# A gated-recurrence and feed-forward kernel on one core: the order of its first loads

## The chip, the cores and the metric

The kernel runs on one core of a Trainium2 chip. The time is device microseconds of that core, from one launch; the median of several runs is given. A core has TensorE for matrix products (its weight loads are counted apart), VectorE and ScalarE for elementwise work, GpSimd, and a sync engine that only issues transfers. ScalarE can issue transfers too, so there are two queues here: the sync queue and the ScalarE queue.

## The reference, cut to what matters

A recurrence with a complex gate for each step and feature, and then a feed-forward layer with a squared ReLU over its output:

```python
# q, k, v, a_re, a_im: (4, 8, 768, 48)    batch, heads, steps, features
mag = np.sqrt(a_re * a_re + a_im * a_im)
scale = np.minimum(mag, 0.999) / (mag + 1e-06)
a_re_n, a_im_n = (a_re * scale, a_im * scale)
for t in range(S):
    new_re = ar * S_re - ai * S_im          # ar, ai: the gates of step t
    new_im = ar * S_im + ai * S_re
    kv = np.einsum('bhd,bhe->bhde', k[:, :, t], v[:, :, t])
    S_re, S_im = (new_re + kv, new_im)
    y[:, :, t] = np.einsum('bhd,bhde->bhe', q[:, :, t], S_re)
...
x = np.ascontiguousarray(attn_out.transpose(0, 2, 1, 3)).reshape(B * S, H * D)   # 3072 x 384
h = np.maximum(x @ w_in, 0.0)               # w_in 384 x 2048
return (h * h @ w_out).astype(np.float32)   # w_out 2048 x 384
```

The weights arrive as 64-bit floats. The kernel gets them as pairs of 32-bit words and makes 32-bit floats of them itself.

## The kernel before, in words

**Tiling.** The steps are cut into 24 chunks of 128, and two chunks of different batches make a group, so there are 12 groups. Features lie on the partitions: the two heads of a pair take 48 partitions each (`rows`), and the 16 partitions left over in each half (`pads`, the gap rows) hold the fourth pair of heads, spread over three columns. So one tile `raw` of 128 partitions by 4 kinds (real gate, imaginary gate, query, key) by 768 holds all of a group. There is one `raw` for all groups: the next group's features can be loaded only when the present group's keys have been read out of it.

**Loads.** `load_parts` (L487) fills `raw`. For each chunk and each half it issues one large transfer into `rows` (L493) and then small ones into the gap rows (L498), one for each of the three columns. For the first group it is called twice, `l0.0` for the gates and `l0.1` for queries and keys, and with `l0.0` the second half goes out on the ScalarE queue (L490). Later groups are loaded whole, on the sync queue. `load_values` (L506) loads the values of a group, two transfers of 192 KB. `fetch` (L593) loads one of 16 blocks of weight words, six transfers for a block of the first weight matrix.

**Work of a group.** `make_operands` (L652) is a list of 22 steps, `o<group>.<step>`. Step 0 squares the gates on ScalarE (L683), and everything in the group follows from that: steps 1 and 2 turn the gates into another order, 4 and 5 take inverse roots, 8 to 11 make the limited gates (VectorE, L735), 6 turns the queries, 12 makes a negated copy on ScalarE (L743), 13 makes the running growth of the keys on VectorE, 14 turns the keys on ScalarE, 15 to 19 run products over blocks of steps on VectorE with some copies on ScalarE (18, the carries, L771), 20 makes the products for TensorE, and 21 copies gap rows to whole heads. `chunk` (L812) then is the recurrence of a chunk (`a` and `b`): scores (L841), keys turned (L848), scores masked by VectorE, sums of values (L867), the new state (L885). `F` and `H` are the first product of the feed-forward layer (L923) and its squared ReLU (L928, L929), `T`, `S`, `Z`, `R` the second (L939, L998), `s` stores.

**Weights.** `W` (`watch`, L580) squares a block of weight words on ScalarE to record its size (L582, L584); `D` (`weights`, L613) decodes it on VectorE in five passes (L569 to L576 and a sum). Three blocks of words can be held at once, so the fourth fetch waits for the first decode.

**The mask.** `turn_mask` (`M0`, L522) copies a triangular mask in another order on ScalarE, transposes it on TensorE and copies it back on ScalarE. Its reader is the masking of the first chunk's scores. Ahead of it on ScalarE stands a single small activation (L557), which brings the table of functions with it.

**Order.** The order on VectorE, TensorE, ScalarE and the sync queue is written out by hand: the string `FRONT` (L1031) names the steps from first to last, `follow` (L1125) carries them out, and each engine keeps that order among its own instructions. An engine whose next instruction waits does nothing behind it; that holds for transfers on a queue as well. GpSimd is not in the hand-written order. [...]

## Time and profile before

| | before |
|---|---|
| time, median of 3 runs | 719.07 us (718.33 to 721.44) |
| span of the profiled execution | 716.5 us |
| TensorE busy with products | 624.1 us (87%) |
| TensorE weight loads | 547.8 us (76%) |
| VectorE busy | 531.7 us (74%) |
| ScalarE busy | 368.6 us (51%) |
| data moved | 47.76 MB, 67 GB/s over the span |
| first squares on ScalarE begin | 18.47 us |
| first use of TensorE for a group | 57.84 us |

A share of the whole span is a mean over stages that have different limits, so the table alone does not say what one change is worth. A profile is read by stage: the slices show where an engine is full and where it is not, and within a stage the idle time before an instruction, with what ended it, shows what it waited for. Where times of a stage are given as three numbers in a row, such as 28.13 of 29.20, they are the busy time and the length of the stage.

### The profile page before, as it was taken

What the parts mean: (1) busy time and instruction counts of PE and PEld (TensorE: products, weight loads), DVE (VectorE), ACT (ScalarE), POOL (GpSimd) and SP (SyncE); (2) the same over time, 40 slices, a digit from 0 to 9 for tenths busy, and PEclk for the clock granted to TensorE, in tenths of its full rate; (3) what the DMA queues carried; (4) which work ended last, traced back from release to release, by engine and by line L of the source; (5) the groups of instructions that cost most, each with busy time, mean ns of one, the idle gap of its engine ahead of it and who ended that gap; (6) DMA issues with size and microseconds to landing.
All of it is one profiled execution on the core that took longest, in us unless ns stands there. A gap on an engine that the chain in (4) does not pass through costs nothing.

```text
span 716.5 us, 12546 instructions
## 1 busy us (share of the span) xinstructions
PE 624.1 (87%) x4955; PEld 547.8 (76%) x4955; DVE 531.7 (74%) x1045; ACT 368.6 (51%) x636; POOL 11.9 (2%) x36
## 2 busy tenths in 40 slices
PE   0005579899979999999999999999999999999995
PEld 0004468676558899998898998988988988989995
DVE  0599999999989697786975886886877868932120
ACT  1729378656536637628347367267276285240230
POOL 3000000000000000000000000000000000000000
PEclk9999789999999999999999999999999999999999
DMA  4596737375070152161331530720620610010101
GB/s 118 101 154 125 101 64 168 93 151 150 21 119 25 22 112 40 31 112 32 66 77 19 91 72 1 117 45 1 116 45 17 116 31 2 10 42 1 28 0 28
DMA packets 46277, 47.76 MB, mean 67 GB/s; under 512 B 6144, under 2 KB 41088, under 8 KB 46208
## 3 DMA queue, kind: packets, MB, share of 16 engines
q1 hardware_dynamic: 45696, 46.46, 33.6%
q8 instruction: 41, 0.67, 0.4%
q10 hardware_dynamic: 512, 0.39, 0.2%
q14 instruction: 28, 0.23, 0.1%
HBM read 36.18 MB, written 4.72 MB: 57 GB/s over the span
## 4 chain that ended last, share of the span: by engine, by line
PE 73%; DVE 13%; DMA 7%; SPq 3%; issue 1%; ACT 1%; ACTq 0%; DVEq 0%
PE h_ps L923 29%; PE o_ps L998 26%; PE a_ps L841 5%; PE o_ps L939 5%; DMA raw<-in_feat_dram 4%; PE y L867 2%; PE y L833 2%; DVE ab L478 2%; PE add L885 2%; PE tp L848 1%; DMA words<-in_moe_w_in_dram 1%; SPq L800 1%; DVE pr L478 1%; DVE w L478 1%; DVE qk L478 1%
## 5 line engine op out<-in xcount | busy, mean ns | idle before, releaser
L923 PE MATMUL h_ps<-x,w 128*128 128x256 f32 x1152 | 261.0, 384 | 8.8 <-DMA x<-x 8.0
L923 PEld LDWEIGHTS h_ps<-x,w 128*128 128x128 f32 x1152 | 219.1, 193 | 39.9 <-DMA x<-x 5.4
L998 PE MATMUL o_ps<-w,h 128*128 128x192 f32 x640 | 110.3, 328 | 0.0
L998 PEld LDWEIGHTS o_ps<-w,h 128*128 128x128 f32 x640 | 104.0, 190 | 2.2 <-issue 1.5
L928 ACT ACTIVATE h<-h_ps 128x512 f32<-128x512 f32 x96 | 57.6, 600 | 89.7 <-PE h_ps L923 86.2
L848 PE MATMUL tp<-ident,qk 128*128 128x128 f32 x120 | 22.2, 297 | 62.9 <-DVE qk L478 54.7
L848 PEld LDWEIGHTS tp<-ident,qk 128*128 128x128 f32 x120 | 14.7, 148 | 68.4 <-ACT size L584 55.0
L478 DVE TENSOR_TENSOR mix<-h 128x256 f32<-128x256 f32 x40 | 16.9, 422 | 62.7 <-ACT h L929 62.7
L929 ACT ACTIVATE h<-h 128x512 f32<-128x512 f32 x96 | 60.6, 631 | 3.0
L663 ACT ACTIVATE qk<-raw 128x768 f32<-128x768 f32 x24 | 36.8, 1534 | 36.0 <-DMA raw<-in_feat_dram 12.6
L998 PE MATMUL o_ps<-w_sum,mix 128*128 128x192 f32 x320 | 54.9, 329 | 0.0
L998 PEld LDWEIGHTS o_ps<-w_sum,mix 128*128 128x128 f32 x320 | 51.8, 190 | 1.4 <-issue 1.4
L478 DVE TENSOR_TENSOR pr<-ab 128x384 f32<-128x384 f32 x84 | 46.8, 557 | 2.3
L478 DVE TENSOR_TENSOR qk<-ab,qk 128x768 f32<-128x768 f32 x48 | 44.9, 956 | 0.8
L939 PE MATMUL o_ps<-w,h 128*128 128x384 f32 x128 | 42.3, 488 | 1.2 <-DVE w L478 0.6
L478 DVE TENSOR_TENSOR a<-a_ps,mask 128x512 f32<-128x512 f32 x48 | 30.9, 685 | 14.7 <-PE a_ps L841 14.7
L841 PE MATMUL a_ps<-qk 48*128 48x128 f32 x576 | 40.7, 291 | 0.0
L663 ACT ACTIVATE both<-z 128x768 f32<-128x768 f32 x24 | 37.1, 1563 | 5.7 <-DVE z L714 5.7
L841 PEld LDWEIGHTS a_ps<-qk 48*128 48x128 f32 x576 | 36.0, 197 | 4.4 <-issue 4.3
L663 ACT ACTIVATE ab<-raw 128x768 f32<-128x768 f32 x24 | 37.7, 1569 | 0.3 <-DVE qk L478 0.3
L939 PEld LDWEIGHTS o_ps<-w,h 128*128 128x128 f32 x128 | 24.2, 190 | 17.5 <-DVE w L478 1.3
L867 PE MATMUL y<-a,vt 128*64 128x128 f32 x384 | 29.0, 285 | 4.5 <-DVE a L478 4.3
(299 smaller groups left out, 817.4 us busy)
## 6 DMA issues: line engine op xcount, KB each, us to landing
raw<-in_feat_dram SPq DMA_DIRECT2D x44, 288.0 KB
words<-in_moe_w_out_dram SPq DMA_DIRECT2D x8, 768.0 KB
last<-qk SPq DMA_DIRECT2D x72, 64.5 KB
vt<-in_vtok_dram SPq DMA_DIRECT2D x24, 192.0 KB
out_dram<-o SPq DMA_DIRECT2D x24, 192.0 KB
raw<-in_feat_dram SPq DMA_DIRECT2D x132, 32.0 KB
words<-in_moe_w_in_dram SPq DMA_DIRECT2D x16, 192.0 KB
words<-in_moe_w_in_dram SPq DMA_DIRECT2D x32, 96.0 KB
```

What stands on the lines that cost most here:

```text
L478: nc.vector.tensor_tensor(out=out, in0=in0, in1=in1, op=op)
L663: nc.scalar.activation(out=out.rearrange("p c j n -> p c n j"), func=AF.Copy, in_=in_.rearrange("p c (n j) -> p c n j", j=L), **kwargs)
L833: nc.tensor.matmul(ys[p_ % 2][crossed(hh, p_), p_ // 2], lhsT=states[b][1 - c_seq % 2][rows(hh), c, p_], rhs=operand(c, p_, rows(hh)), sta ...
L841: nc.tensor.matmul(ps[hh][:, p_], lhsT=operand(2 + c, p_, rows(hh)), rhs=operand(c, p_, rows(hh)), start=(c == RE), stop=(c == IM))
L848: nc.tensor.transpose(tp[:, g], operands[gi][:, 2 + c, b, g, 0:C], ident)
L867: nc.tensor.matmul(tiles["y"][p_ % 2][crossed(hh, p_), p_ // 2], lhsT=v[:, at:at + ROWS], rhs=tiles["am"][hh][:, p_], start=(first and p_ ...
L885: nc.tensor.matmul(add[rr, c, p_], lhsT=kt[c][:, p_, rr], rhs=v[:, at:at + D], start=True, stop=True)
L923: nc.tensor.matmul(ps[:, j], lhsT=w1[:, g, (2 * f + j) * P:(2 * f + j + 1) * P], rhs=x_of[i][:, g], start=(g == 0), stop=(g == NG - 1))
L928: nc.scalar.activation(out=h, in_=h_ps[i, f], func=AF.Relu)
L929: nc.scalar.activation(out=h, in_=h, func=AF.Square)
L939: nc.tensor.matmul(o_of[i, b], lhsT=tokens_of(i, f, b)[:, j], rhs=w2[:, k], start=(k == 0), stop=(k == NFB - 1))
L998: nc.tensor.matmul(to, lhsT=x(k)[:, j], rhs=factor(z)[:, 2 * k + j], start=(z in (0, 1, 3) and k == j == 0), stop=(k == KH // 2 - 1 and j ...
```

## The change

The gates of the first group are to be first of all on both queues. For this the order string begins with `l0.0` in place of `M0`; the table's activation becomes `M0`, behind the transfers of `l0.0` on ScalarE, and the mask becomes `M1`, put behind the turned queries. The values of the first two groups, `v0` and `v1`, move behind the first fetch of weights. And the gap rows are loaded in as few transfers as the kinds and the columns allow: with two kinds asked for there are two transfers, one for each kind, in place of three, one for each column; with four kinds there are three as before. The rest of the order string is the same.

```diff
                     in_=feat[n, hh, :, parts, 0:NG].rearrange("d x g t -> d x (g t)"))
-                rest = feat[n, hh].rearrange("(r g) x p t -> g r x p t", g=NG)
-                for g in range(NG):
-                    queue.dma_start(out=raw[pads(hh), parts, b, g],
-                                   in_=rest[g, :, parts, NG])
+
+                gap = raw[pads(hh), parts, b]
+                rest = feat[n, hh].rearrange("(r g) x p t -> r x g p t", g=NG)[:, parts, :, NG]
+                for i in range(min(gap.shape[1:3])):
+                    at = (slice(None), i) if gap.shape[1] < NG else (slice(None), slice(None), i)
+                    queue.dma_start(out=gap[at], in_=rest[at])
...
-    def turn_mask():
+    def turn_mask(step):
+        if step == 0:
+
+            nc.scalar.activation(out=sums[:, 0:1], in_=tiny, func=AF.Abs_reciprocal_sqrt)
+            return
         nc.scalar.copy(out=mask.rearrange("p (j n) -> p n j", j=L),
                        in_=plain.rearrange("p (n j) -> p n j", j=L))
...
-    nc.scalar.activation(out=sums[:, 0:1], in_=tiny, func=AF.Abs_reciprocal_sqrt)
...
-        "M0 l0.0 v0 v1 l0.1 o0.0 o0.3 o0.1 o0.4 o0.5 o0.7 o0.2 f0 o0.8 o0.10 o0.9 o0.11 o0.6 W0 "
-        "f1 o0.13 o0.12 o0.15 o0.14 l1 o0.16 W1 o0.17 f2 D0 o0.18 o0.19 o1.6 o0.20 o1.0 f3 W2 "
-        "a0.1 o1.3 o1.1 o0.21 D1 o1.4 o1.5 o1.2 a0.2 o1.7 f4 a0.0 W3 D2 o1.8 o1.9 a0.3 a0.5 "
+        "l0.0 M0 l0.1 o0.0 o0.3 o0.1 o0.4 o0.5 o0.7 o0.2 f0 v0 v1 o0.8 o0.10 o0.9 o0.11 o0.6 M1 "
+        "W0 f1 o0.13 o0.12 o0.15 o0.14 l1 o0.16 W1 o0.17 f2 D0 o0.18 o0.19 o1.6 o0.20 o1.0 f3 "
+        "W2 a0.1 o1.3 o1.1 o0.21 D1 o1.4 o1.5 o1.2 a0.2 o1.7 f4 a0.0 W3 D2 o1.8 o1.9 a0.3 a0.5 "
...
-        "M": lambda _: turn_mask(),
+        "M": turn_mask,
```

## The prediction

> **What bounds the kernel now.** I read three views, in this order: the page's slices, to find where TensorE is not yet busy; the busy times by stage, to see which engine sets the pace of that stage; and the timeline of the start, to see what the pacing engine waits for.

> ```profile
> PE   0005579899979999999999999999999999999995
> DVE  0599999999989697786975886886877868932120
> DMA  4596737375070152161331530720620610010101
> ```

> Each digit is the busy share of one slice of 17.9 us. TensorE does nothing for three slices and is near full from the tenth on; VectorE is full from the third slice; in the first slice nearly nothing runs, and the DMA is busy less than half.

> The stages, in the columns PE, PEld, DVE, ACT, POOL, then granted clock, DMA share and GB/s:

> ```profile
> 0.00:18.40 18.40, 0.48 (x1) 0.18 (x1) 0.38 (x6) 2.15 (x4) 6.11 (x24) 1.00 0.42 116
> 18.40:28.60 10.20, 0.00 (x0) 0.00 (x0) 2.89 (x4) 9.54 (x10) 0.00 (x0) 1.00 0.81 160
> 28.60:57.80 29.20, 0.00 (x0) 0.00 (x0) 28.13 (x54) 12.83 (x23) 0.00 (x0) 1.00 0.71 114
> 57.80:91.20 33.40, 18.78 (x172) 15.35 (x172) 32.08 (x66) 20.77 (x40) 0.24 (x1) 0.86 0.68 113
> 240.00:716.50 476.50, 468.77 (x3834) 427.99 (x3830) 330.00 (x700) 230.62 (x403) 3.55 (x8) 1.00 0.25 47
> ```

> So there are four regimes, one after the other. To 18.4 us no engine works and data is awaited. From 18.4 to 28.6 ScalarE is busy 9.54 of 10.20 us. From 28.6 VectorE is, 28.13 of 29.20 and 32.08 of 33.40 us, and it stays so to about 154. From 240 on TensorE is, 468.77 of 476.50. A delay at the very start is handed through all of them. The timeline of the start (start, duration, engine, line, tiles; in brackets the idle time before it and its releaser; SPq and ACTq are transfers being issued):

> ```profile
> 0.81 0.39 SPq L493 DMA_DIRECT2D raw<-in_feat_dram  x1
> ...
> 3.16 0.37 ACT L527 COPY mask<-turned 128x128 f32<-128x128 f32 x1 [0.57 <-PE turned L526]
> ...
> 4.52 2.78 SPq L508 DMA_DIRECT2D vt<-in_vtok_dram  x4
> 5.39 0.39 ACTq L493 DMA_DIRECT2D raw<-in_feat_dram  x1
> ...
> 8.65 4.95 ACTq L498 DMA_DIRECT2D raw<-in_feat_dram  x3
> ...
> 13.64 0.44 ACTq L493 DMA_DIRECT2D raw<-in_feat_dram  x1
> 14.12 1.89 ACTq L498 DMA_DIRECT2D raw<-in_feat_dram  x3
> ...
> 18.47 1.48 ACT L683 ACTIVATE sq<-raw 128x1536 f32<-128x1536 f32 x1 [14.93 <-DMA raw<-in_feat_dram]
> ...
> 28.59 0.96 DVE L735 SCALAR_TENSOR_TENSOR both<-both 128x768 f32<-128x768 f32 x1 [3.60 <-ACT both L663]
> ...
> 29.66 0.88 ACT L582 ACTIVATE size<-words 128x768 bf16<-128x768 f32 x1
> ...
> 31.59 0.75 ACT L743 ACTIVATE ab<-ab 128x672 f32<-128x672 f32 x1
> ...
> 54.03 1.48 ACT L683 ACTIVATE sq<-raw 128x1536 f32<-128x1536 f32 x1 [2.75 <-DVE ab L478]
> ```

> The reader is to see that the first squares, at 18.47, waited 14.93 us for the gates (real and imaginary parts), and why these were late. The sync queue's half was issued from 0.81 on. The ScalarE queue's half was issued from 5.39 to 16.0, because that queue first had to finish the mask (3.53), and then found the value transfers and the queries and keys ahead of it. [...]

> [...] a gap transfer of 16 KB issued at 15.69 is what the squares at 18.47 wait for, 2.8 us for 16 KB. [...] the trace has the load at 1.28 us (0.81 to 2.09), and the activation follows at 2.10, [...] the trace shows a granted clock of 0.50 from 84 to 92 us, after TensorE had little to do.

> **The change, part by part.** *Order of the start.* The gates' 12 transfers (4 of 147 kB, 8 of 24.6 kB, 786 kB in all) are now first on both queues. By the issue pace of the sync queue (0.42 + 0.04 us each) four leave on each queue from 0.81 to 2.6; [...] In the view by single microseconds the DMA moved 23, 154, 80, 121 and 16 kB in the stretches from 1 to 6 us: 394 kB, which is the sync queue's half, 393 kB. So data starts about 1.9 us after the start. For the rate I take 180 GB/s (181, 183 and 176 GB/s at 8 to 11 us; about the same at 22 to 29): 786 kB take 4.4 us and end at 6.3. The tail to the landing is not shown for this order. It lies between nothing and the 2.4 us from the end of the last gap's issue (16.01) to the squares; I take 0.9, since the last gap transfers are issued some 1 us before the other data has passed. Squares at 7.2 us; 6.5 to 8.7 by the tail, 9.6 if the rate is only the 116 GB/s of the first stage (6.8 + 1.9 + 0.9). Gain 18.47 - 7.2 = 11.3 us.

> *Table load and first activation* now follow the six issues of the ScalarE queue. These end at about 5.0 [...], so the load ends at 6.3 and the activation at 6.5, under the last data's 7.2. Cost 0; at worst 0.5 if the sixth issue is late.

> *Fewer small transfers.* For the first group the gap rows take 2 instead of 3 transfers per half, chunk and pair of kinds: 8 fewer of 0.46 us on the queues and 8 fewer places. That is inside the 7.2 above for the gates; the queries' and keys' data ends at 1.9 + 1573 / 180 = 10.6, landed at about 12. They are wanted at 28.35 - 11.3 = 17.1: hidden. Later groups still use 3.

> *The mask* moves behind the queries and ahead of the first watch of weights. It costs 0.39 + 0.57 + 0.37 = 1.3 us on ScalarE (rows L523 and L527 with the wait for the transpose), and TensorE is idle then. Behind it on ScalarE stand the watch and the negated copy, which ran from 29.66 to 32.34; VectorE wants the negated copy only at 35.15. Slack 2.8, cost 1.3: hidden, 1.5 us left. The mask's own reader is at 68.46.

> *The values* go behind the first block of weights. Their first reader is the product at 69.20 (57.9 after the shift), and they land before 25. Hidden. Behind them on the sync queue stand the second block of weights and then the second group's features. Features, values and two blocks are 3.93 MB; at 180 GB/s from 1.9 us they end at 23.7, landed near 25. The second watch wants its block at 36.59 - 11.3 = 25.3, and what stands behind it on ScalarE (the carries) is wanted only at 45.35 - 11.3 = 34.0. The first block (1.9 + 2359 / 180 = 15.0, landed at 16 to 17) is wanted at 29.66 - 11.3 + 1.3 = 19.7.

> *The second group's features* wait for the keys' turned copy, which frees the tile: 36.81 before, 25.5 after. By then the earlier data is just done, where before the DMA stood idle from 30 to 36.8. If it is 2 us late, the slack of 2.75 us at 54.03 (its squares waited for VectorE, not for the features) takes it. From here on issue and work are tied to VectorE's own progress, so the whole schedule moves by 11.3. Sum: 719.07 - 11.3 + 0 = 707.8 us.

> **The rivals.** *Likeliest, full shift:* for it, ScalarE and VectorE are busy 94 to 96% from the squares on and TensorE's late stage is full, so nothing else binds. 707.8 us.
> *Part is eaten by the next data wait:* the first 30 us now need 3.93 MB without the pause that was there. If the squares start at 9.6 (116 GB/s), 8.9 us is gained; another 1 to 2 us could go to late blocks or late features beyond the 2.75 us of slack. 719.07 - 8.9 + 1.5 = 711.7 us. Against it: 160 GB/s were moved from 18.4 to 28.6.
> *Hidden anyway:* weights, not gates, pace the front, and VectorE meets them at the same time as before. 719 us. For it: DMA is at its limit around 38 to 56 us. Against it: up to 130 us one watch waited 0.4 us for weights, and their fetches are released by VectorE, so they move too.
> *Slower:* the second watch, behind the values, blocks ScalarE so long that the carries come late, or a half-clock stretch (the trace has 13.7 us of one, by the granted clocks from 80 to 96 us) falls elsewhere, over busy matmuls: up to 6.8 us. With the gain lost as well, 719 + 5 = 724 us. To undo the gain by the watch alone the second block would have to land near 43 us, 18 later than worked out.

> **How the numbers follow.** Full shift 0.70, part eaten 0.19, hidden 0.07, slower 0.04. The range has the full shift with its bounds (squares 6.5 to 8.7 and about 1.5 us of spread between runs, 718.33 to 721.44 before) and most of the part-eaten case: 705 to 712.5. Half a per cent is 3.6 us, so the first two cases are faster: 0.89; hidden gives the same, 0.07; slower 0.04.

> **What would show it.** Right: both queues' gate issues begin at 0.8; squares near 7; the gates' product on VectorE near 17.3; the first keys' transpose on TensorE near 46.5; the gap to the old trace stays at 11 us in the TensorE stage. Wrong: squares after 10; VectorE waits for the negated copy or for the second group's squares; a watch that holds ScalarE until the carries; a new half-clock stretch.

## The result, and the profile after

The changed kernel takes 712.27 us (median of 4 runs, 708.89 to 712.48) against 718.70 us (4 runs, 717.95 to 721.44): a ratio of 0.9893, 95% interval 0.9853 to 0.9932. Run again on a second chip it takes 707.77 us (6 runs, 707.17 to 711.85) against 719.94 us (27 runs), a ratio of 0.9833 [0.9805, 0.9861]. Both intervals lie clear of 1, so it is faster; but two medians of one program differ by 4.5 us. Most of what follows is about that: the early gain is the one that was worked out, within 0.6 us, and something later gives or takes 4 us.

Line numbers of the changed kernel are 3 to 4 higher than before from the gap rows' loads on (these are L501, were L498; the squares are L687, were L683), and the table's activation is L527, was L557. First the page's slices, one digit for each 17.8 us. PEclk, the granted TensorE clock in tenths, was not shown for before; its line there is `PEclk9999789999999999999999999999999999999999`.

```profile
PE   0025689999979999999999999999999999999995
...
DVE  1999989999798787996966886877868968932120
...
PEclk9999699999879999999999999999999999999998
DMA  5885582853351061341430620720611610010101
```

VectorE is full one slice earlier than before, and the DMA's second slice is an 8 where it was a 5. New is a dip of PEclk in slices 11 and 12, about 190 to 215 us, where before it is 9 throughout. The same four regimes, in the columns of the prediction (PE, PEld, DVE, ACT, POOL, clock, DMA share, GB/s):

```profile
0.00:7.00 7.00, 0.00 (x0) 0.00 (x0) 0.38 (x6) 1.49 (x2) 6.10 (x24) 1.00 0.48 125
7.00:18.00 11.00, 0.00 (x0) 0.00 (x0) 3.05 (x4) 9.69 (x10) 0.00 (x0) 1.00 0.59 132
18.00:47.00 29.00, 0.47 (x1) 0.18 (x1) 27.93 (x54) 13.54 (x25) 0.00 (x0) 1.00 0.92 164
229.00:711.00 482.00, 473.78 (x3909) 431.96 (x3907) 332.83 (x704) 235.29 (x411) 3.30 (x9) 0.99 0.25 47
```

The empty first regime has shrunk from 18.4 to some 7 us. The next two are as long and as full as they were: from the squares to the gates' product on VectorE it is 10.10 us, was 10.12 (the window of ScalarE, 9.69 of 11.00, begins 0.7 us before the squares), and VectorE is busy 27.93 of 29.00. The DMA share of the third went from 0.71 to 0.92, as the pause from 30 to 36.8 us (DMA share 0.00, the end of a wait of 10.2 us of the sync queue for ScalarE's turned keys) is gone. The timeline of the start of the changed kernel:

```profile
0.81 0.43 ACTq L493 DMA_DIRECT2D raw<-in_feat_dram  x1
...
4.17 1.21 ACTq L501 DMA_DIRECT2D raw<-in_feat_dram  x2
...
5.42 1.28 ACT L527 ACT_TABLE_LOAD   x1 [5.42 <-issue]
6.71 0.20 ACT L527 ACTIVATE sums<-tiny 128x1 f32<-128x1 f32 x1
7.72 1.48 ACT L687 ACTIVATE sq<-raw 128x1536 f32<-128x1536 f32 x1 [0.81 <-DMA raw<-in_feat_dram]
...
17.82 0.96 DVE L739 SCALAR_TENSOR_TENSOR both<-both 128x768 f32<-128x768 f32 x1 [3.59 <-ACT both L667]
...
22.07 0.75 ACT L747 ACTIVATE ab<-ab 128x672 f32<-128x672 f32 x1
...
29.19 0.90 ACT L586 ACTIVATE size<-words 128x768 bf16<-128x768 f32 x1 [3.17 <-DMA words<-in_moe_w_in_dram]
...
34.57 0.34 ACT L775 COPY carry<-ab 128x180 f32<-128x180 f32 x1 [3.34 <-DVE ab L478]
...
43.26 1.48 ACT L687 ACTIVATE sq<-raw 128x1536 f32<-128x1536 f32 x1 [1.60 <-DVE ab L478]
```

The squares begin at 7.72 instead of 18.47 us, 10.75 earlier, and the last data is the only thing they wait for, 0.81 us after the activation is done. The first turned keys on TensorE come at 47.10 instead of 57.87, 10.77 earlier. Their lines in the two timelines, before first, with the products that follow in the changed kernel:

```profile
57.87 0.87 PE L848 MATMUL tp<-ident,qk 128*128 128x128 f32 x3 [54.74 <-DVE qk L478]
...
47.10 0.87 PE L852 MATMUL tp<-ident,qk 128*128 128x128 f32 x3 [27.24 <-DVE qk L478]
47.90 2.93 PE L845 MATMUL a_ps<-qk 48*128 48x128 f32 x24
```

Followed product by product through both traces, TensorE is ahead of before by

```
at (us of before)   58 to 90       100     110    190    200    210    240 to the end
ahead by (us)       10.6 to 11.3   11.2    9.2    9.3    8.2    5.3    6.0
```

So the lead holds to 90 us, and then 1.5 us go near 105 and over 3 us near 205. In both places (95 and 196 us in the changed kernel) the granted clock falls to 0.50. One window of 3.41 us just ahead of the second place, and one within it, in the trace of the changed kernel:

```profile
186.14:189.55 3.41, 1.69 (x16) 0.90 (x18) 3.38 (x8) 1.23 (x4) 0.00 (x0) 1.00 0.36 91
...
192.97:196.38 3.41, 3.41 (x25) 2.52 (x25) 1.49 (x3) 0.65 (x2) 0.00 (x0) 0.50 1.02 177
```

TensorE has 1.69 us of work in the first (it waits for VectorE, 3.38 busy), and then runs at half clock while it has work all the time. The granted clock was 0.50 in these stretches (start and length in us, the one after the last product left out):

```
before                     81.9 (13.65)                215.1 (3.41)
changed                    70.1 (13.65)  94.0 (3.41)   189.6 (10.24)  210.0 (3.41)
changed, second profile    70.4 (13.65)  94.3 (3.41)   189.8 (6.83)   206.9 (6.83)
```

The stretch at 81.9 lies for the most part where TensorE has little to do (busy 4.65 of its first 10.24 us), and its counterpart in the changed kernel is at 70.1 (6.83 of 13.65). The others lie over busy products: TensorE is busy throughout those of the changed kernel, and 2.92 of 3.41 us in the one at 215.1 of before. The first products are slow in both kernels, too: the 24 products at 47.90 above take 2.93 us, as they do at 58.67 before, and the same kind of batch takes 1.61 us later (at 231.67, and before at 108.16). That they ran at half clock is an estimate, from such a batch that took 2.94 us at a granted 0.50 (further down): the profile has no record of the clock until 63.3 us (before: 75.1), so the 1.00 that it shows up to there is no measurement.

### The profile page after: what moved, and what is told of

It reads as the page before. It is cut to its first block, busy times and chain, and to the rows that moved or that the text cites. A ratio compares the mean times of both kernels' runs of the same rounds, so it can differ in the third digit from the quotient of the medians.

```text
span 710.7 us, 12538 instructions
## 1 busy us (share of the span) xinstructions
PE 629.6 (89%) x4955; PEld 551.7 (78%) x4955; DVE 531.9 (75%) x1045; ACT 368.6 (52%) x636; POOL 11.2 (2%) x36
## 4 chain that ended last, share of the span: by engine, by line
PE 77%; DVE 14%; DMA 4%; SPq 2%; issue 1%; ACT 0%; DVEq 0%; ACTq 0%
PE h_ps L927 31%; PE o_ps L1002 26%; PE a_ps L845 6%; PE o_ps L943 5%; PE y L871 3%; PE y L837 3%; DVE ab L478 3%; PE add L889 2%; PE tp L852 2%; DVE pr L478 2%; DVE decoded L575 1%; DVE decoded L580 1%; DVE qk L478 1%; DVE w L478 1%; DVE sq L753 1%
## 5 line engine op out<-in xcount | busy, mean ns | idle before, releaser
L932 ACT ACTIVATE h<-h_ps 128x512 f32<-128x512 f32 x96 | 57.6, 600 | 91.8 <-PE h_ps L927 88.8
L478 DVE TENSOR_TENSOR mix<-h 128x256 f32<-128x256 f32 x40 | 16.9, 422 | 62.5 <-ACT h L933 62.5
L667 ACT ACTIVATE qk<-raw 128x768 f32<-128x768 f32 x24 | 36.8, 1532 | 35.1 <-DMA raw<-in_feat_dram 14.4
L478 DVE TENSOR_TENSOR pr<-ab 128x384 f32<-128x384 f32 x84 | 46.7, 556 | 2.3
L478 DVE TENSOR_TENSOR qk<-ab,qk 128x768 f32<-128x768 f32 x48 | 44.9, 956 | 0.8
L478 DVE TENSOR_TENSOR a<-a_ps,mask 128x512 f32<-128x512 f32 x48 | 30.9, 685 | 17.8 <-PE a_ps L845 17.8
L845 PEld LDWEIGHTS a_ps<-qk 48*128 48x128 f32 x576 | 36.8, 200 | 4.6 <-issue 4.5
L943 PEld LDWEIGHTS o_ps<-w,h 128*128 128x128 f32 x128 | 24.1, 190 | 17.9 <-DVE w L478 1.5
```

Source lines behind the costliest of these rows:

```text
L478: nc.vector.tensor_tensor(out=out, in0=in0, in1=in1, op=op)
L667: nc.scalar.activation(out=out.rearrange("p c j n -> p c n j"), func=AF.Copy, in_=in_.rearrange("p c (n j) -> p c n j", j=L), **kwargs)
L845: nc.tensor.matmul(ps[hh][:, p_], lhsT=operand(2 + c, p_, rows(hh)), rhs=operand(c, p_, rows(hh)), start=(c == RE), stop=(c == IM))
L932: nc.scalar.activation(out=h, in_=h_ps[i, f], func=AF.Relu)
L943: nc.tensor.matmul(o_of[i, b], lhsT=tokens_of(i, f, b)[:, j], rhs=w2[:, k], start=(k == 0), stop=(k == NFB - 1))
```

## The experiments

Two questions: does the lead at 47 us come from the parts as worked out, and are the half-clock stretches what takes it back? The rivals for the loss: the changed loads themselves delay something later (a wait for data or for a buffer), or the runs simply scatter.

**The changed kernel again, on another chip.** No edit.

> The changed kernel itself, unedited, for the clock of each run. Half-clock theory (the gain at the start is 10.8 us, and TensorE at half clock around 95 and 190 us takes some 5 us back): runs differ, and the longer a run the lower its mean granted clock; 708 to 713 us, with each us of half clock in the late stretch costing about 0.4 us. Rival, data (late weights and the outputs' store take the gain back): all runs alike near 712 us, with no relation to the clock.

Measured: 707.77 us (711.28, 707.17, 707.21, 711.85, 707.61, 707.93). The six fall into two groups 4 us apart, and the granted clock recorded with each run goes with them: 0.983 to 0.986 for the four near 707.4, 0.975 and 0.972 for 711.28 and 711.85. The 27 runs of the kernel before beside them do the same:

```
                                clock 0.980 and over         below 0.980
kernel before, this chip        718.60 us (15 runs)          721.92 us (12 runs)
changed kernel, this chip       707.41 us (4 runs)           711.57 us (2 runs)
difference                      11.2                         10.35
kernel before, three chips      718.77 us (36 runs)          722.27 us (45 runs)
changed kernel, all ten runs    707.61 us (5 runs)           712.09 us (5 runs)
```

At like clock the change is worth 10.2 to 11.2 us. The first comparison had drawn three of four changed runs from the low group, and of the four runs before only one (721.44 us) lies in that group's range. So the loss is no property of the changed loads: the kernel before pays 3.5 us in about half of its runs too. (No trace shows one of those runs of before; that stretches are what they pay for is argued from their clock.) That the clock does it, and doesn't just go with it, needs runs in which it is kept up.

**Products that keep the clock up**, added to both kernels. A token `w` in the order string multiplies the identity by itself into a PSUM tile that nobody reads, where TensorE had been waiting; the computation is otherwise complete. There are 116 products in all (the expectations say 111), in batches of 5 to 30:

```diff
-        "b0.7 a0.9 b0.1 o1.16 b0.2 b0.3 g0 b0.4 o1.17 b0.8 v2 b0.9 o1.18 o1.19 o2.6 F0.0 o1.20 "
+        "b0.7 a0.9 w30 b0.1 o1.16 b0.2 w5 b0.3 g0 b0.4 o1.17 w5 b0.8 v2 b0.9 o1.18 o1.19 o2.6 w26 F0.0 o1.20 "
...
+    def warm(n):
+        if not warm_ps:
+            warm_ps.append(po.tile([P, DM], F32, tag="o", name="warm"))
+        for _ in range(n):
+            nc.tensor.matmul(warm_ps[0][:, 0:P], lhsT=ident, rhs=ident, start=True, stop=True)
```

> The changed kernel with 111 more small products of the identity on TensorE, in the waits where its clock fell; no result uses them. Half-clock theory: no half clock between 60 and 215 us in the trace, the shift against the kernel before stays near 10.8 us to the end, 706 to 708 us. Rival, data: the same losses of 1.5 us near 105 and 4 us near 200, 712 us or a little more by the added products.

> The kernel before with the same added products, as a control. Half-clock theory: it has few and short half-clock stretches on its critical path, so it gains at most 2 us, 717 to 719 us, and lies 10 to 11 us behind the changed kernel with added products. Rival, data: 719 us, and 6 to 7 us behind.

Measured: 710.85 us (710.38 to 713.07) with the change, 721.65 (721.12 to 722.34, 22 runs) without it; clocks 0.994 to 0.998 in all of them, and no half-clock stretch in either trace from the clock's first record, at 62 and 75 us, to the last product. The two medians differ by 10.8 us, and the two traces by 10.7 from the first keys (46.94 and 57.61) to the end. But the medians lie some 3 us over the top of what I expected. At least one batch was too long. A line of the changed kernel's timeline with 16 added products (32 instructions, as each is run as two):

```profile
92.50 3.74 PE L1108 MATMUL warm<-ident 128*128 128x128 f32 x32
```

They fill 3.74 us in a wait that was 2.32 us in the changed kernel, and the work behind them is late. So the test shows that the lead is kept when the clock is, and nothing on how much a kept clock brings.

**Fewer products, then fitted ones.** The same edit with batches of 14, 2, 2, 13, 7, 4 and 11 (53 products), and with 14, 2, 2, 21, 9, 9 and 12 (69).

> The changed kernel with 53 added products instead of 111, so that each batch is shorter than the wait it stands in. Half-clock theory: no half clock between 60 and 215 us, no delay by the added products, and the late shift against the kernel before is the early one, 10.8 us: 707 to 708 us in every run, a spread under 1.5 us. Rival, data: runs from 707 to 712 us as without the products.

> The kernel before with the same 53 products. Half-clock theory: 718 us in every run, the fast end of the kernel before, and 10.5 to 11 us behind the changed kernel with the products. Rival, data: 718 to 722 us as without.

> The changed kernel with 69 added products, each batch fitted to the wait in which it stands (14, 2, 2, 21, 9, 9 and 12). Half-clock theory: no half clock between 60 and 215 us, no delay over 0.5 us, 707 to 708.5 us with a spread under 2 us in all runs, 10.5 to 11 us ahead of the same products in the kernel before. Rival, data: runs up to 712 us stay.

> The kernel before with the same 69 products. Half-clock theory: 718 to 719.5 us with a spread under 2 us, the runs of 721 to 724 us of the kernel before are gone. Rival, data: 718 to 724 us as without.

Measured: with 53 products 708.40 (706.99 to 712.38) and 721.08 us (718.54 to 723.11); with 69 products 709.25 (707.31 to 710.29) and 721.49 us (718.20 to 723.45). The spreads I expected, under 1.5 and under 2 us, were missed: stretches turned up at other places (at 91.8 and 201.1 us in the trace of the kernel before with 53). With 69 products the runs of the kernel before lie at 718.20 to 719.33 us when the clock was 0.996 or more and at 721.32 to 723.45 when it was 0.993 or less, with none between. With 53 they do not sort so cleanly: at a clock of 0.989 to 0.991 they lie anywhere from 719.70 to 723.11. A run's mean clock also counts stretches in which TensorE has little to do, like the one at 81.9 us of before. Nor did the products make the kernel before faster: its medians with and without them are 721.08 and 721.42 us, and 721.49 and 721.92. The two profiled runs with 69 products had no stretch between 71 us and the last product, and in them the change is nearly a rigid shift: 11.29 us early, 11.0 to 11.5 us from 95 us on, 11.26 at the end. That is the forecast's picture, and in these runs it rules out the rival that the changed loads delay something later.

**The same two programs once more.** No edit.

> The changed kernel with the 69 products once more, for a second trace, since the runs of it still spread from 707.3 to 710.3 us. Half-clock theory: a run of 709 us or more shows a half-clock stretch after 85 us, and one of 707 to 708 us shows none. Rival, another cause for the spread: 709 us or more at full clock from 85 us on.

> The kernel before with the 69 products once more: 718 to 719.5 us with full clock from 85 us on, or 720 us or more with a half-clock stretch there. Rival: 720 us or more at full clock.

Measured: 711.90 and 718.49 us. The first is the most telling run of the study: it is the same program as the one of 707.31 us above, and from 85 to 226 us the two traces agree within 0.16 us, product by product. Then one has a stretch of 10.24 us and is 4.9 us behind, 4.6 at the end. Windows of the run of 707.31 us:

```profile
221.31:224.72 3.41, 3.06 (x33) 2.10 (x32) 1.15 (x3) 2.98 (x7) 0.00 (x0) 1.00 0.60 95
224.72:228.14 3.42, 2.19 (x38) 2.05 (x40) 2.10 (x4) 3.39 (x7) 0.19 (x1) 1.00 0.15 23
```

And of the run of 711.90 us:

```profile
222.93:226.35 3.42, 1.85 (x36) 1.26 (x35) 1.19 (x3) 3.36 (x9) 0.09 (x1) 1.00 0.47 73
226.35:229.76 3.41, 3.41 (x36) 3.08 (x29) 1.92 (x2) 2.86 (x4) 0.10 (x1) 0.50 0.02 5
```

In each trace the starts and ends of stretches lie on one grid of 3.41 us (those of the changed kernel begin at 70.09, 93.98, 189.55 and 210.03 us, the last three 7, 35 and 41 times 3.41 us after the first); I call one interval of it a step. On the grid of the slower run a step ends at 226.35, and its work is 1.85 us, because TensorE waits 1.40 us for a transfer there. On the grid of the faster run (counted from its one stretch, at 67.7) the same pause is split between two steps, with 3.06 and 2.19 us of work, and nothing happens. The price, in the timeline of each run, the faster first (start, duration, engine, line, tiles):

```profile
226.50 1.61 PE L845 MATMUL a_ps<-qk 48*128 48x128 f32 x24
...
229.55 2.86 PE L927 MATMUL h_ps<-x,w 128*128 128x256 f32 x12
```

```profile
226.83 2.94 PE L845 MATMUL a_ps<-qk 48*128 48x128 f32 x24
...
232.42 4.90 PE L927 MATMUL h_ps<-x,w 128*128 128x256 f32 x12
```

The same 24 products take 1.61 and 2.94 us, and the same twelve 2.86 and 4.90. Here the falling clock is the cause of the loss and not only its companion: everything ahead of it was alike.

**Three transfers for the gap rows of the first group, as before; all else changed.**

```diff
-                for i in range(min(gap.shape[1:3])):
-                    at = (slice(None), i) if gap.shape[1] < NG else (slice(None), slice(None), i)
-                    queue.dma_start(out=gap[at], in_=rest[at])
+                for g in range(NG):
+                    queue.dma_start(out=raw[pads(hh), parts, b, g],
+                                   in_=rest[g, :, parts, NG])
```

> The changed kernel with three transfers instead of two for the gap rows, as before. Theory that places are what counts: 4 more transfers on the gates' way at about 0.5 us each on two queues, squares at 8.7 to 9.7 us instead of 7.7, the first keys' transpose 1 to 2 us later than 47.1. Rival, bytes: squares stay within 0.3 us of 7.7.

```profile
8.43 1.48 ACT L685 ACTIVATE sq<-raw 128x1536 f32<-128x1536 f32 x1 [1.11 <-DMA raw<-in_feat_dram]
```

(Its lines are 2 lower than the changed kernel's.) Measured: squares at 8.43, 0.71 us later than with two, a little under what I expected; first keys 0.71 later too (47.81). Its lead of 10.05 us over before lasts to the end, and its time, 708.22 us at a clock of 0.986, is 10.6 under the 718.77 of like runs of before.

**The mask ahead of the gates again; all else changed.**

```diff
-        "l0.0 M0 l0.1 o0.0 o0.3 o0.1 o0.4 o0.5 o0.7 o0.2 f0 v0 v1 o0.8 o0.10 o0.9 o0.11 o0.6 M1 "
+        "M0 M1 l0.0 l0.1 o0.0 o0.3 o0.1 o0.4 o0.5 o0.7 o0.2 f0 v0 v1 o0.8 o0.10 o0.9 o0.11 o0.6 "
```

> The changed kernel with the table's activation and the mask again ahead of the gates on the ScalarE queue. Theory that this queue's late start counted: its half leaves from 3.6 us on instead of 0.8, and the sync queue's queries and keys get places and bytes ahead of it; squares at 10 to 11 us, first keys' transpose at 49.5 to 50.5. Rival, only the values counted: squares within 0.5 us of 7.7.

```profile
5.26 0.41 ACTq L493 DMA_DIRECT2D raw<-in_feat_dram  x1
...
14.12 1.48 ACT L687 ACTIVATE sq<-raw 128x1536 f32<-128x1536 f32 x1 [10.58 <-DMA raw<-in_feat_dram]
```

Measured: squares at 14.12 us, where I had expected 10 to 11, and first keys at 53.48, so the place of the table load and the mask is 6.38 of the 10.77 us. The ScalarE queue's gates begin to be issued 4.45 us later than in the changed kernel, but the squares are 6.4 later: the sync queue goes on meanwhile to queries and keys, and the gate transfers behind the first leave only at 7.31, 9.19 and 9.81. Whether those queries and keys cost the gates turns on the queues or bytes, this run does not separate. It took 718.31 us at a clock of 0.977, level with before as it was first measured, in spite of 4.39 us of lead at 53.5: its trace has stretches of 10.24 and 3.41 us at 195.1 and 215.6. Against the low group of before, 722.27 us, its lead is 4.0.

**The values ahead of queries and keys again; all else changed.**

```diff
-        "l0.0 M0 l0.1 o0.0 o0.3 o0.1 o0.4 o0.5 o0.7 o0.2 f0 v0 v1 o0.8 o0.10 o0.9 o0.11 o0.6 M1 "
+        "l0.0 M0 v0 v1 l0.1 o0.0 o0.3 o0.1 o0.4 o0.5 o0.7 o0.2 f0 o0.8 o0.10 o0.9 o0.11 o0.6 M1 "
```

> The changed kernel with the values of two groups again right behind the gates. Theory that the gates' own issue decides: they hold their places by then, squares at 7.7 to 8.5 us; queries, keys and the first block of weights come 4.4 us later (786 kB at 180 GB/s), so the first watch waits 1 to 2 us on ScalarE, and the first keys' transpose is at 47.1 to 49. Rival, the values held the gates back: squares at 11 us or later.

```profile
7.00 1.48 ACT L687 ACTIVATE sq<-raw 128x1536 f32<-128x1536 f32 x1 [0.19 <-DMA raw<-in_feat_dram]
...
22.93 0.90 ACT L586 ACTIVATE size<-words 128x768 bf16<-128x768 f32 x1 [2.93 <-DMA words<-in_moe_w_in_dram]
...
25.66 0.56 DVE L478 TENSOR_TENSOR pr<-ab 128x384 f32<-128x384 f32 x1 [1.92 <-ACT ab L747]
```

Measured: the gates are even earlier, squares at 7.00 (why, stays open), but the first block of weights is late. The first watch then holds ScalarE for 2.93 us, the negated copy behind it is late, and VectorE waits 1.92 us for it. First keys at 48.36, so the values' place is worth 1.26 us, through a wait of weights and not of gates. The time was 708.73 us at a clock of 0.984.

The three parts undone singly cost 6.38, 1.26 and 0.71 us, 8.35 of 10.77. Each is read from one trace. In six traces with the whole change, added products or not, the first keys lie at 46.71 to 47.10 us, and in five without it at 57.41 to 58.00, so each figure is good to some 0.4 us, and all three runs lie outside that range. The parts may share places and waits, which would explain the rest; no run undid two together. No version tried is clearly better than the changed kernel.

## Why the prediction was right or wrong

*Order of the start: right, 0.55 us too short.* Squares were forecast at 7.2 and begin at 7.72, so the gain is 10.75 and not 11.3. The term that was too small is the tail of 0.9 us: the data came as fast as forecast (748 kB had begun to move by 6.0 us, the first queries' part included, for 786 by 6.3; from 2 to 6 us, with both queues in use, it was 182 GB/s). That the fifth and sixth issue would come later than the first four was my estimate: the ScalarE queue's fourth ends at 3.22 and its fifth begins at 4.17. What held it there was not shown; on the sync queue the trace shows 0.4 us of waits for earlier feature transfers up to 8 us, and in the kernel before, up to 20 us, 4.0 us for values and 1.8 for features. The ScalarE queue's sixth issue ends at 5.38 (forecast 5.0), and the squares follow 2.34 us later. That is the 2.4 us between last issue and squares seen before, which I had as the upper bound and thought to be shorter. The gates' product (17.82 for 17.3) and the first keys (47.10 for 46.5) carry these 0.5 us on.

*Table load and activation: right.* They end at 6.91, under the data's 7.72.

*Fewer small transfers: some 0.7 us.* I had no figure of its own for it, only "inside the 7.2".

*The mask: right.* With it in its new place the negated copy starts at 22.07 and VectorE's next step at 24.39 does not wait for it. The run with the mask in front shows that its old place was the largest part.

*The values: right in kind.* The second block of weights landed at 29.2, some 4 us after my 25, so its watch waited 3.17 us. The rate of 180 GB/s that I took to hold throughout was 132 GB/s from 7 to 18 us. What stands behind, the carries, still waited 3.34 us for VectorE at 34.57: hidden by a slack found in the profile. My step gave the move no gain of its own; it has one of 1.26 us, by letting the first block come in time.

*The second group's features: right.* Of the slack of 2.75 us ahead of its squares 1.60 is left: its turned queries, which waited for a transfer, came at 40.12, only 9.62 us earlier than before, and the slack took the 1.15 us by which they were late.

*"So the whole schedule moves by 11.3": failed in the traced run, held in others.* It holds to the end in the pair of traces without stretches over busy products (11.3), with three gap transfers (10.05), and at like clock (11.2 and 10.2 between medians). The five changed runs at 0.981 to 0.986 have a median of 707.61 us, for 707.8 forecast; that this is so close is partly luck, as the sum started from 719.07, a median of runs from both groups. The step fails for the median of the first comparison, 712.27, where 6.4 us of the 11.3 are left. That this still lies in the range, which ended at 712.5, is luck too: the range reached so far for the part-eaten case, which did not happen. The cause in the traces is what my fourth rival named, a half-clock stretch that "falls elsewhere, over busy matmuls: up to 6.8 us"; by the medians of the two groups it cost 3.5 (before) to 4.5 us (changed) a run. I put it at 0.04 and tied it to a lost gain. It belongs beside every case instead, as a draw made anew in each run, of the kernel before too: the 718.33 to 721.44 us that I called spread were, by their times, these two groups.

*Part eaten by the next data wait: not so*, though 711.7 us is near the first median. In the trace of the changed kernel the lead is whole at 90 us, long after the late block at 29. *Hidden anyway: no*, the gates paced the front.

The half-clock stretches in the traces are 3.41, 6.83, 10.24 and 13.65 us long, on a grid of 3.41 us whose place differs between two runs of one program (in the two windows of runs with 69 products above, steps end at 224.72 and at 226.35 us, 1.63 apart). Steps with up to 1.99 us of work out of 3.41 were followed by half clock, so a step need not be empty for it. What stays open is the exact limit, and whether the grid's place alone decides in the runs that have no trace.

## What to carry to other kernels

Look at what the first instruction of the pacing engine waits for, and give that data the first places on every queue: a table load and one small computation ahead of half the gates on one queue cost 6.4 us here, 4.45 us by which the queue started later and some 2 more, as the other queue's later data went ahead meanwhile. A delay at the start of a chain of full engines came back one for one at the end (11.29 us early and 11.26 at the end, in the pair of traces without stretches over busy products), but before a median is read, sort the runs by their granted clock, since a draw with three of four runs from the low group on one side and, by its time, one of four on the other hid over 4 us of an 11 us gain. A pause of 1.4 us on TensorE cost 4.6 us by the end in one run, and none of it in another run of the same program.
